# First tile of a two-layer convolution: plain load, TensorE transposes and a tap-by-tap product in place of transposing DMAs and product sums, with the shifts moved to ScalarE and a delayed GELU

## The chip, the cores and the metric

One core of a Trainium2 chip. The metric is the device time of the program in microseconds (us); every run here was in the fast state of the chip, so all runs may be compared. A profiled run also has a span, from the first to the last counted instruction, which is about 2 us shorter than its time. "Granted clock" is the share of TensorE's full clock that the records of the chip show for a stretch or a whole run.

Short names: PE is TensorE's matmul, PEld its weight load, DVE VectorE, ACT ScalarE, POOL GpSimd, SP an engine that here only issues DMAs. PSUM is the memory into which TensorE writes its products and from which VectorE and ScalarE read them. `L302` is line 302 of the kernel; a helper that issues all matmuls has one line, so tiles and operand names tell matmuls apart.

## The reference, cut to what matters

```python
# x: (2, 4000, 512), w1, w2: (5, 512, 512), g: (2, 8, 512), all bf16
h = sum(einsum("btc,cd->btd", pad(x)[:, i:i+T], w1[i]) for i in range(5))
h = gelu(h)[:, ::2]                      # only every second sample is kept
f = sum(einsum("btc,cd->btd", pad(h)[:, i:i+T1], w2[i]) for i in range(5))
f = gelu(f)[:, ::2]                      # (2, 1000, 512)
j = tanh((f @ w_f)[:, :, None] + (g @ w_g)[:, None])
out = j @ w_o                            # (2, 1000, 8, 512)
```

Both convolutions have five taps and stride 2. The kernel holds the samples in four phases, `xs[r]` with r = 0 to 3, where column c of phase r is sample 4c + r; one column then gives two outputs, sample 4c and sample 4c + 2. Direct, those two outputs take ten products (five taps each). The kernel takes seven: sums and differences of phases (a0, a1, a2, a3, b1, b3, and b2, which is phase 1 itself) are multiplied with taps or sums of taps, and the results are combined afterwards. Input channels come in four blocks of 128. A unit is 128 output channels of one tile: 28 matmuls in product form, 40 tap by tap. A tile has four units. The *epilogue* of a unit in product form is what VectorE and ScalarE do with its products: a copy that releases a PSUM bank (release copy), two combining operations, a pair sum and the GELU.

## The kernel before: what the change touches

```python
for ph in (2, 3, 1, 0):                     # first samples: DMA transposes of DRAM
    load_x(0, ph, 16, 272)
...                                         # cut: the other loads
def xf(src, off, dst, c0, n, which, eng):   # operands of the product form
    ph = lambda r, d: src[r, :, off + d:off + d + n]
    o = lambda kind: dst[kind, :, c0:c0 + n]
    if which == "a0":   tt(eng, o(0), ph(2, -1), ph(2, 0), sub)   # ph(2, -1): shifted
    elif which == "b3": tt(eng, o(3), ph(3, 0), ph(1, 0), sub)
    elif which == "b1": tt(eng, ph(3, -1), ph(3, -1), ph(1, 0), sub)
    elif which == "a3": tt(eng, o(2), ph(0, 1), ph(0, 0), sub)
    elif which == "a1": tt(eng, o(1), ph(0, 0), ph(2, 0), add)
    elif which == "a2": tt(eng, ph(0, 0), ph(2, 0), ph(0, 0), sub)
...
nxt = [(w, "pool" if w == "a3" else "dve") for w in ("b3", "a0", "b1", "a3", "a1", "a2")]
...
def post(self, m, where, between=()):       # after the matmuls of unit m
    act(c, ps.cols(C, n), ACT.Copy, scale=0.5)                    # release copy
    ...                                     # cut: two scalar_tensor_tensor on VectorE
    for f in between: f()                   # operands of the next tile
    tt("dve", tv, tv, ps.pair(A, step, n), add)                   # pair sum
    ...
    act(o, tv, ACT.Gelu_apprx_tanh)         # GELU follows at once
...
tiles = [Tile_(1, 0, xs[0], 16, ..., 250), Tile_(1, 0, xs[0], 266, ..., 250),
         Tile_(1, 0, xs[1], 12, ..., 250), Tile_(1, 0, xs[1], 262, ..., 250),
         Tile_(1, 1, xs[2], 16, ..., 500), Tile_(1, 1, xs[0], 12, ..., 500)]   # layer 1
```

Layer 1 is four tiles of 250 columns for batch 0 and two of 500 for batch 1; layer 2 is two tiles of 500. The rest (two projections, tanh, the output product) is the same in both kernels. PSUM has eight banks. A 250-column unit takes two of them and a 500-column unit four, handed out in turn by a counter `count["unit"]`. Helpers record every operation in program order and put in the waits; each engine runs its own operations in that order.

## Time and profile before

| | before |
|---|---|
| time, median (range, runs) | 314.73 us (314.15 to 315.94, 4) |
| span of the profiled run, granted clock | 312.4 us, 0.955 |
| chain that ended last: TensorE, VectorE, "issue" | 74%, 12%, 6% |
| TensorE busy | 280.3 us |
| second tile's first matmul; third tile; batch 1; layer 2 | 39.67; 55.03; 84.77; 137.88 us |

The page of the kernel before gives busy time (x is the number of instructions), then the span in 40 slices of 7.8 us, where a digit is the busy share in tenths (9 is 90% or more) and PEclk the granted clock in tenths.

```profile
PE 280.3 (90%) x1487; PEld 148.1 (47%) x1498; DVE 197.8 (63%) x262; ACT 128.4 (41%) x179; POOL 58.6 (19%) x41
...
PE   8259179959959999999998999999999999999995
...
POOL 1745000060199994004000000000000000000000
PEclk9959769998979999999999999999999999999999
...
PE 74%; DVE 12%; issue 6%; DMA 3%; ACT 3%; SPq 1%; DVEq 0%; ACTq 0%
```

TensorE is full from slice 13 on, at about 94 us. The holes, and the low clock, are all in the first third. The same stretch in windows (start:end, length, busy time of PE, PEld, DVE, ACT and POOL, granted clock, DMA share, GB/s):

```profile
8.28:18.78 10.50, 1.87 (x16) 1.49 (x17) 4.74 (x3) 0.00 (x0) 9.11 (x2) 0.80 1.12 264
18.78:34.00 15.22, 13.50 (x96) 10.67 (x96) 14.91 (x20) 0.38 (x1) 4.45 (x3) 0.80 1.14 184
34.00:42.65 8.65, 1.85 (x9) 1.04 (x9) 5.49 (x13) 2.75 (x6) 0.00 (x0) 0.56 0.81 172
42.65:54.90 12.25, 12.25 (x103) 10.73 (x104) 7.85 (x17) 3.74 (x8) 0.12 (x1) 0.89 0.20 45
54.90:68.00 13.10, 9.61 (x87) 8.04 (x85) 9.31 (x15) 2.80 (x6) 5.77 (x2) 1.00 1.00 263
68.00:89.00 21.00, 18.48 (x148) 15.11 (x148) 13.65 (x22) 4.76 (x10) 3.89 (x2) 0.92 0.39 113
```

The first number after the length is TensorE. From 8.28 to 18.78 us it worked 1.87 of 10.50 us, with 16 matmuls; from 34.00 to 42.65 it worked 1.85 of 8.65 us, at a clock of 0.56. VectorE, on the other hand, was busy 14.91 of 15.22 us in the second row: it was the engine that the first tile waited for. In the chain of waits of the same kernel the first 18 us read (start, us, what):

```profile
4.60 9.25 DMA xs_49<-in_x_dram
...
13.94 3.96 DVE xt_54 L283
```

So the second operand (b3, which needs two further phases; a0 was made at 7.45 us) had to wait for the transposing DMAs, 9.25 us of the chain, and the VectorE operation that makes it took 3.96 us beside GpSimd; one of the same size took 0.69 us without it. The timeline shows that stretching again at the first 500-column tile (start, us, engine, line, operation, operands and sizes, and in brackets how long the engine had been idle and what ended it):

```profile
83.53 1.19 DVE L283 TENSOR_TENSOR xt_54<-xs_51 128x2000 bf16<-128x2000 bf16 x1
...
85.11 3.52 POOL L283 TENSOR_TENSOR xt_55<-xs_49 128x2000 bf16<-128x2000 bf16 x1 [17.63 <-PE acc L294]
...
87.03 2.65 DVE L283 TENSOR_TENSOR xs_51<-xs_51 128x2000 bf16<-128x2000 bf16 x1
...
89.78 1.82 PE L294 MATMUL acc<-xs_51,w_t 128*128 128x500 bf16 x4 [3.14 <-issue]
```

A subtraction of 2000 bf16 elements takes VectorE 1.19 us. Started under a GpSimd operation it took 2.65 us: if it waited until GpSimd was done at 88.63, it then took 1.05 us, near its usual time. TensorE waited 3.14 us here; the profile names no releaser, but these matmuls read what the operation writes, and they start 0.10 us after its end. The Trainium skill, "SBUF — State Buffer", section "Who interferes with whom", says that a VectorE instruction with two SBUF inputs contends with a GpSimd instruction that reads SBUF, and that the one that comes second is blocked, not slowed. This trace agrees here. (The 3.96 us operation above ended 1.2 us before the record of the GpSimd operation beside it, so that case doesn't tell.)

### The profile page before, as it was taken

To read this page: it belongs to the slowest core of one execution; us is meant where nothing else is said; L and a number is where in the kernel's file an instruction comes from. 1 tells how busy PE (TensorE), PEld (TensorE's weight loads), DVE (VectorE), ACT (ScalarE), POOL (GpSimd) and SP (SyncE) were. 2 spreads that over 40 slices of the span, in tenths; PEclk is the share of its full clock that TensorE was granted. 3 is DMA by queue.
4 is the path that set the end of the run, shared out by engine and by line. 5 is a ranking of instruction groups with operands and counts; after the bars stand their busy time and mean duration, and the time that the engine had idled before them with its cause. 6 is when DMAs were issued, how large, how long until landed. Compare 5 with 4: busy or idle time off the path is not lost.

```text
span 312.4 us, 4021 instructions
## 1 busy us (share of the span) xinstructions
PE 280.3 (90%) x1487; PEld 148.1 (47%) x1498; DVE 197.8 (63%) x262; ACT 128.4 (41%) x179; POOL 58.6 (19%) x41
## 2 busy tenths in 40 slices
PE   8259179959959999999998999999999999999995
PEld 3147159848824434444443444444444444444442
DVE  0299775666678776768674324656767676767674
ACT  1000223221311223231324344876786786793840
POOL 1745000060199994004000000000000000000000
PEclk9959769998979999999999999999999999999999
DMA  8999940997000000000000000224444445444444
GB/s 220 297 183 177 228 106 3 201 342 200 2 0 1 0 2 0 0 2 0 1 0 2 0 0 0 69 81 154 153 153 152 148 147 162 151 153 151 151 153 135
DMA packets 58641, 31.87 MB, mean 102 GB/s; under 512 B 35950, under 2 KB 58622, under 8 KB 58622
## 3 DMA queue, kind: packets, MB, share of 16 engines
q1 hardware_dynamic: 55982, 29.00, 34.4%
q10 hardware_dynamic: 2640, 2.62, 2.7%
q8 instruction: 12, 0.20, 0.3%
q14 instruction: 7, 0.06, 0.1%
HBM read 6.82 MB, written 16.38 MB: 74 GB/s over the span
## 4 chain that ended last, share of the span: by engine, by line
PE 74%; DVE 12%; issue 6%; DMA 3%; ACT 3%; SPq 1%; DVEq 0%; ACTq 0%
PE acc L294 74%; DMA xs_49<-in_x_dram 3%; DVE xt_54 L283 2%; DVE w_t L283 1%; SPq L324 1%; DVE ty_65 L283 1%; DVE ty_66 L432 1%; DVE xs_49 L283 1%; ACT jT L287 1%; DVE ty_66 L283 1%; DVE ty_65 L432 1%; DVE xt_55 L283 1%; DVE w_sb L283 1%; ACT cs_64 L287 1%; DVE ty_67 L283 1%
## 5 line engine op out<-in xcount | busy, mean ns | idle before, releaser
L294 PE MATMUL acc<-wo_sb,jT 128*128 128x512 bf16 x489 | 107.5, 379 | 0.6
L294 PEld LDWEIGHTS acc<-wo_sb,jT 128*128 128x128 bf16 x500 | 48.8, 98 | 59.1 <-DVE ty_66 L283 0.3
L294 PE MATMUL acc<-xt_54,w_sb 128*128 128x250 bf16 (+1 forms) x256 | 50.6, 338 | 0.6 <-DVE xt_54 L283 0.6
L294 PE MATMUL acc<-xt_55,w_sb 128*128 128x250 bf16 (+1 forms) x256 | 49.6, 328 | 1.5 <-DVE xs_50 L283 1.3
L287 ACT ACTIVATE jT<-feT_77,geT 128x1000 bf16<-128x1000 f32 (+6 forms) x44 | 35.8, 890 | 0.0
L294 PEld LDWEIGHTS acc<-xt_54,w_sb 128*128 128x128 bf16 x256 | 26.4, 103 | 18.6 <-issue 2.1
L287 ACT ACTIVATE jT<-feT_76,geT 128x1000 bf16<-128x1000 f32 (+4 forms) x40 | 35.1, 948 | 0.0
L294 PEld LDWEIGHTS acc<-xt_55,w_sb 128*128 128x128 bf16 x256 | 25.4, 100 | 18.3 <-DVE xs_50 L283 1.6
L294 PE MATMUL acc<-xs_49,w_t 128*128 128x250 bf16 (+1 forms) x96 | 18.0, 316 | 9.3 <-DVE xt_54 L283 6.3
L294 PE MATMUL acc<-xs_49,w_sb 128*128 128x250 bf16 (+1 forms) x48 | 10.4, 364 | 8.6 <-DVE xs_49 L283 8.6
L287 ACT ACTIVATE cs_63<-acc 128x250 f32<-128x250 f32 (+1 forms) x16 | 7.5, 467 | 22.9 <-PE acc L294 22.9
L294 PEld LDWEIGHTS acc<-xs_49,w_t 128*128 128x128 bf16 x96 | 9.3, 100 | 14.9 <-DVE xt_54 L283 6.6
L283 DVE TENSOR_TENSOR xt_54<-xs_49 128x1000 bf16<-128x1000 bf16 x7 | 7.8, 1141 | 13.3 <-DMA xs_49<-in_x_dram 13.3
L573 DVE CAST ost_79<-acc 128x512 bf16<-128x512 f32 x11 | 7.6, 691 | 10.3 <-PE acc L294 10.3
L573 DVE CAST ost_85<-acc 128x512 bf16<-128x512 f32 x10 | 6.9, 692 | 10.4 <-PE acc L294 10.4
L432 DVE SCALAR_TENSOR_TENSOR ty_66<-acc,cs_64 128x250 f32<-128x250 f32 (+1 forms) x12 | 6.0, 544 | 11.1 <-ACT cs_64 L287 11.1
L287 ACT ACTIVATE ost_90<-acc 128x512 bf16<-128x512 f32 x10 | 6.0, 597 | 16.4 <-PE acc L294 16.4
L287 ACT ACTIVATE hT_61<-ty_65 128x500 bf16<-128x500 f32 x6 | 3.9, 658 | 21.0 <-DVE ty_65 L283 21.0
L432 DVE SCALAR_TENSOR_TENSOR ty_65<-acc,cs_63 128x250 f32<-128x250 f32 (+1 forms) x12 | 6.0, 542 | 9.5 <-ACT cs_63 L287 9.5
L294 PE MATMUL acc<-xs_51,w_t 128*128 128x500 bf16 x32 | 8.9, 404 | 3.1 <-issue 3.1
L294 PE MATMUL acc<-xs_50,w_t 128*128 128x250 bf16 x64 | 9.7, 274 | 2.1 <-DVE xt_55 L283 2.1
L379 POOL TENSOR_SCALAR w_t<-w_t 128x2048 bf16<-128x2048 bf16 x2 | 11.6, 5783 | 0.2
(98 smaller groups left out, 354.7 us busy)
## 6 DMA issues: line engine op xcount, KB each, us to landing
w_sb<-in_w_dram ACTq DMA_DIRECT2D x5, 512.0 KB, 7.7
w_sb<-in_w_dram SPq DMA_DIRECT2D x5, 512.0 KB, 6.4
out_dram<-ost_79 SPq DMA_DIRECT2D x11, 128.0 KB, 1.9
out_dram<-ost_83 SPq DMA_DIRECT2D x11, 128.0 KB, 1.9
out_dram<-ost_81 SPq DMA_DIRECT2D x10, 128.0 KB, 1.9
out_dram<-ost_87 SPq DMA_DIRECT2D x10, 128.0 KB, 1.9
out_dram<-ost_80 SPq DMA_DIRECT2D x9, 128.0 KB
out_dram<-ost_82 SPq DMA_DIRECT2D x9, 128.0 KB
```

The lines of the kernel that those rows point to most:

```text
L283: pl.op(eng, lambda e: e.tensor_tensor(out=o.ap, in0=a.ap, in1=b.ap, op=op), (a, b), (o,))
L287: pl.op("act", lambda e: e.activation(o.ap, i.ap, func, scale=scale, bias=0.0 if bias is None else bias.ap), rd, (o,))
L294: ins = e.matmul(o.ap, lhsT=l.ap, rhs=r.ap, start=start and n == 0, stop=stop and n == len(pairs) - 1, skip_group_check=not check)
L324: pl.dma("sp", lambda e: e.dma_start_transpose(out=dst.ap, in_=src), (), (dst,))
L379: pl.op(eng, lambda e: e.tensor_scalar(out=v.ap, in0=v.ap, scalar1=2.0, scalar2=None, op0=ALU.mult), (v,), (v,))
L432: pl.op("dve", lambda e, o=o, f=f: e.scalar_tensor_tensor(out=o.ap, in0=d.ap, scalar=f, in1=c.ap, op0=ALU.mult, op1=add), (d, c), (o,))
L573: pl.op("dve", lambda e, o=o, v=v: e.tensor_copy(out=o.ap, in_=v.ap), (v,), (o,))
```

## The change

The intent is to fill the first 138 us. Six things change together.

1. The first 256 columns come by a plain DMA, 128 groups of four samples at a time. TensorE transposes them in 32 steps into PSUM, and VectorE and ScalarE copy them out.
2. The first tile is convolved tap by tap (160 matmuls instead of 112), so it needs neither operands nor sums of weights nor an epilogue. VectorE makes the weight sums meanwhile.
3. The shifted operands a0, a3 and b1 are first copied by ScalarE (`shift`), so that VectorE reads aligned data. GpSimd no longer makes a3.
4. Batch 0's second half is one tile of 500 columns instead of two of 250.
5. The GELU of a unit is recorded after the next unit's release copy (`flush`).
6. GpSimd's preparation of layer 2's weights is cut into quarters, one recorded behind each unit of batch 1's first tile.

Smaller things come with these: the weights are loaded in the order of the taps, later samples are loaded only after the first ones, and b3 instead of b1 is the operand that is written in place.

The core of the diff; hunks and parts of hunks are left out where `# cut` stands.

```diff
+        first = [load_xr(rt) for rt in range(2)]
+        for i in (0, 4, 2, 1, 3):
+            load_w("act", w1_sb[i], w1[i].rearrange("(k c) d -> c k d", c=P))
# cut
-        warm_mm(22)
+        warm_mm(NWARM)        # NWARM = 16
+        psb = ps.h[:, :].bitcast(BF16)
+        for rt in range(2):
+            for pp in range(2):
# cut: bank 4 + 2 * rt + pp, eight transposes e.transpose(..., ident)
+                if pp:
+                    act(o, pv, ACT.Copy)
+                else:
+                    pl.op("dve", lambda e, o=o, pv=pv: e.tensor_copy(out=o.ap, in_=pv.ap), (pv,), (o,))
# cut
+        def shift(src, off, dst, c0, n, which):
+            r, d, kind = {"a0": (2, -1, 0), "a3": (0, 1, 2), "b1": (3, -1, 3)}[which]
+            act(dst[kind, :, c0:c0 + n], src[r, :, off + d:off + d + n], ACT.Copy)
# cut
-                tt(eng, o(0), ph(2, -1), ph(2, 0), sub)
+                tt("dve", o(0), o(0), ph(2), sub)
# cut: a3 and b1 alike
+                tt("dve", ph(3), ph(3), ph(1), sub)      # b3, now in place
# cut
-        count = {"unit": 0}
+        count = {"unit": 2}
# cut
                 act(c, ps.cols(C, n), ACT.Copy, scale=0.5)
+                flush()
+                for f in scal:
+                    f()
# cut
                 tt("dve", tv, tv, ps.pair(A, step, n), add)
-                act(o, tv, ACT.Gelu_apprx_tanh)
+                pending.append(lambda: self.gelu(m, tv))
# cut
-                 Tile_(1, 0, xs[1], 12, xt[1], 0, 500, 250), Tile_(1, 0, xs[1], 262, xt[1], 250, 750, 250),
+                 Tile_(1, 0, xs[1], 12, xt[1], 0, 500, 500),
# cut
+        for i in (0, 4, 2, 1, 3):
+            for m in range(NK):
+                for s in range(2):
+                    r, d = tap_at[i][s]
+                    mm(ps.cols(m * NT + 256 * s, n),
+                       [(w1_sb[i, k, m * P:(m + 1) * P], xs[0][r, k, 16 + d:16 + d + n]) for k in range(NK)],
+                       i == 0 and s == 0, i == 3, False)
# cut: weight sums on VectorE
+        for w in ("a0", "b1", "a3"):
+            tiles[1].shift(w)
+        for w in ("a0", "b1", "b3", "a3", "a1", "a2"):
+            tiles[1].xf(w)
```

## The prediction

> **What bounds it now.** The chain of waits gives TensorE 74% of the 312.4 us span, but windows show two halves. At the end TensorE is busy 109.6 of 113.4 us; a 500-column unit of 28 matmuls takes 5.9 us. From layer 2's start (137.9 us in the timeline) to the end is 174.5 us, which the change hardly touches. The first 137.9 us hold only four 500-column tiles (94.5 us). About 43 us are lost: 30 until the second tile starts (39.7/42.65 us: eight DMA transposes issuing over 16.8 us, 12 VectorE weight sums of 0.69 us, VectorE operations stretched to 2.2 us beside GpSimd), 7.5 to 84.8 us, 6 to 137.9 us.
>
> The Trainium skill, "TensorE: Matmul & The Clock Gate", "Part 1: The HAM clock gate", says the array drops to half clock after an idle window of about 3.4 us, until one busy window. The trace agrees: granted clock 0.50 from 16 to 24 and 36 to 44 us, and even after a 2.1 us gap at 66 us.
>
> **What changes, costed (estimates from the trace).**
> - First samples: 1 MB plain beside the weights. DMA moved 232-360 GB/s from 2 to 12 us, so they land at 7-9 us; 16 transposes (1-1.7 us) and a 1.1-1.2 us copy follow. Convolution starts near 11 us.
> - Tap by tap: 160 matmuls of 250 columns instead of 112: 17.1 instead of 12 us, plus about 2 at half clock, as TensorE has holes from 6 to 11 us. Ends at 29-30 us. Weight sums run under it. No VectorE epilogue: four GELUs of 0.65 us.
> - Second tile: in-place b3 writes cells that the last tap reads, so b3, a3, a1 (0.6-0.7 us each) run only after the convolution: a gap near 2.1 us and probably a slow window (+1.7). Starts near 32 us.
> - It needs VectorE for 4 x 1.4 + 6 x 1.19 = 12.8 us against 12 us of TensorE, and ScalarE shifts of 1.95 us (0.83 ns per element) precede the next copy. The third tile, now 500 columns, takes PSUM banks just used, so I expect 2-3 us of stall and another slow window. It starts at 47-48 us.
> - Then three tiles at 23.6 us. GpSimd leaves the operands; its weight preparation (about 24 us) still runs beside VectorE, which has about 43 of 47 us in those tiles: 1-2 us of stall.
> - Delayed GELU and ScalarE copies: 12.6 of 23.6 us of ScalarE per 500-column tile, off the path. Aligned VectorE operands gain nothing: shifted and unshifted subtractions both take 0.6-0.69 us.
>
> **Sum.** 47.5 + 1.7 + 3 x 23.6 + 1 = 121 us for layer 2's start instead of 137.9; plus 174.5 gives a 295.5 us span, about 297 us as time (2.1 more). Without the two stalls and slow windows: 289. I say 295 us, range 288 to 302.
>
> **What would show it.** First convolution matmul at 10-12 us; its 160 matmuls over 17-20 us; then a VectorE-caused gap of about 2 us; VectorE-caused idling before the third tile; layer 2's first matmul at 115-124 us; from there 174-175 us.
>
> **What would make it wrong.** Plain loads landing after 10 us, or taps 1 and 3 after their turn; half clock through most of the tap-by-tap convolution (up to +8 us); transposed loads for the third tile arriving after 48 us; contention with GpSimd or ScalarE's order delaying 500-column tiles; or the transition stalls hidden (289 or less). A result within 2% would need about 13 us more of losses.
>
> Faster by over 2%: 0.94; within 2%: 0.05; slower: 0.01.

## The result, and the profile after

The changed kernel takes 292.55 us (290.94 to 293.93, 4 runs) against 314.73 us: a ratio of 0.9289, with a 95% interval of 0.9233 to 0.9344. A ratio here is the mean time of one kernel's runs over that of the other's of the same rounds, so not quite the ratio of the medians quoted.

The profiled run of the changed kernel is the slowest of its four, 293.93 us, with a span of 292.1 us and a clock of 0.988. Its page, the same lines:

```profile
PE 280.4 (96%) x1460; PEld 141.6 (48%) x1460; DVE 182.3 (62%) x237; ACT 158.0 (54%) x187; POOL 33.1 (11%) x39
...
PE   8897987999999999999989999999999999999995
...
POOL 1000000099994000000000000000000000000000
PEclk9999797999999999999999999999999999999999
...
PE 92%; DVE 3%; issue 2%; ACT 1%; POOL 0%; DVEq 0%; ACTq 0%; POOLq 0%
```

TensorE was busy as long as before (280.4 us) in a span 20 us shorter. Its share of the chain rose from 74% to 92%. Two dips are left, at slices 5 and 7 of the PEclk row. The windows (columns as before) show what they are:

```profile
0.00:9.91 9.91, 7.43 (x49) 3.88 (x49) 1.98 (x3) 3.42 (x4) 1.50 (x18) 1.00 0.83 289
9.91:27.23 17.32, 17.31 (x160) 15.50 (x160) 9.98 (x15) 4.88 (x6) 0.00 (x0) 1.00 1.17 237
27.23:29.25 2.02, 0.01 (x1) 0.01 (x1) 1.89 (x4) 0.59 (x1) 0.00 (x0) 1.00 1.01 225
29.25:33.00 3.75, 3.75 (x20) 2.76 (x21) 1.22 (x3) 1.05 (x2) 0.00 (x0) 0.54 1.15 164
33.00:43.04 10.04, 10.03 (x95) 8.97 (x92) 8.70 (x13) 6.80 (x8) 0.12 (x1) 1.00 0.69 143
43.04:45.62 2.58, 0.00 (x1) 0.01 (x1) 2.52 (x5) 0.66 (x1) 0.00 (x0) 1.00 0.46 106
45.62:50.00 4.38, 4.38 (x13) 1.71 (x14) 0.00 (x0) 1.53 (x3) 0.00 (x0) 0.61 1.50 210
50.00:118.15 68.15, 68.15 (x325) 31.48 (x323) 50.77 (x53) 33.19 (x31) 31.46 (x20) 1.00 0.24 68
```

The tap-by-tap convolution ran from 9.91 to 27.23 us without a hole and at full clock. Then TensorE stood still for 2.02 us while VectorE was busy for 1.89 of them, and worked the next 3.75 us at a clock of 0.54. The same happened once more at the third tile: 2.58 us still, then 4.38 us at 0.61. From 50.00 to 118.15 us it was busy all of 68.15 us. A stretch of low clock ("slow window" below) costs 3.75 x (1 - 0.54) = 1.7 us, or 4.38 x (1 - 0.61) = 1.7 us.

The timeline names what ended the two gaps, and shows the two ScalarE copies out of PSUM, which end at 9.81 us, 0.10 before the convolution's first matmul (VectorE's two, 0.69 us each, were done by 9.01):

```profile
7.87 1.94 ACT L295 ACTIVATE xs_49<-acc 128x1024 bf16<-128x1024 bf16 x2 [1.32 <-PE acc L363]
...
29.25 1.00 PE L302 MATMUL acc<-xs_49,w_t 128*128 128x250 bf16 x4 [2.02 <-DVE xt_54 L291]
...
44.89 0.67 DVE L291 TENSOR_TENSOR ty_67<-ty_67,acc 128x500 f32<-128x500 f32 x1
45.62 1.15 PE L302 MATMUL acc<-xs_50,w_t 128*128 128x500 bf16 x4 [2.58 <-DVE ty_67 L291]
```

The first gap waits for operands of the second tile (`xt_54`), the second for the last pair sum of the second tile (`ty_67`), which still reads a PSUM bank that the third tile wants. These two waits are the subject of the first three experiments.

Where the 20.3 us of the span went, from the first matmuls of each stage in the two timelines:

| stretch | before | after | saved |
|---|---|---|---|
| start to the end of the second tile's matmuls | 55.03 | 43.04 | 12.0 |
| from there to the first matmul of batch 1 | 29.74 | 27.89 | 1.9 |
| batch 1 of layer 1, to layer 2's first matmul | 53.11 | 47.22 | 5.9 |
| layer 2 to the end | 174.5 | 173.95 | 0.6 |

Two 500-column tiles are 224 matmuls; the 47.22 us of the third row are what TensorE needs for them alone (0.21 us each at full clock). Nothing is left to gain in that row. What remains are the two gaps with their slow windows, and the start.

### The profile page after: what moved, and what is told of

It reads as the page before. It is cut to its first block, busy times and chain, and to the rows that moved or that the text cites. A ratio compares the mean times of both kernels' runs of the same rounds, so it can differ in the third digit from the quotient of the medians.

```text
span 292.1 us, 3892 instructions
## 1 busy us (share of the span) xinstructions
PE 280.4 (96%) x1460; PEld 141.6 (48%) x1460; DVE 182.3 (62%) x237; ACT 158.0 (54%) x187; POOL 33.1 (11%) x39
## 4 chain that ended last, share of the span: by engine, by line
PE 92%; DVE 3%; issue 2%; ACT 1%; POOL 0%; DVEq 0%; ACTq 0%; POOLq 0%
PE acc L302 92%; ACT xt_55 L295 1%; DVE ty_69 L291 1%; PE acc L363 1%; DVE xt_54 L291 0%; DVE xt_55 L291 0%; DVE ty_68 L486 0%; DVE ost_86 L626 0%; DVE ty_67 L291 0%; DVE ty_68 L291 0%; DVE ty_69 L486 0%; DVE ty_67 L486 0%; POOL zero L288 0%; ACT cs_65 L295 0%; ACT cs_66 L295 0%
## 5 line engine op out<-in xcount | busy, mean ns | idle before, releaser
L302 PE MATMUL acc<-xt_55,w_sb 128*128 128x500 bf16 x160 | 38.3, 374 | 0.0
L302 PE MATMUL acc<-xt_54,w_sb 128*128 128x500 bf16 (+1 forms) x160 | 33.8, 347 | 0.0
L295 ACT ACTIVATE cs_65<-acc 128x500 f32<-128x500 f32 (+1 forms) x12 | 6.6, 553 | 37.8 <-PE acc L302 37.8
L302 PE MATMUL acc<-xs_49,w_sb 128*128 128x250 bf16 (+1 forms) x192 | 23.7, 278 | 1.2 <-issue 1.2
L302 PEld LDWEIGHTS acc<-xt_55,w_sb 128*128 128x128 bf16 x160 | 15.7, 98 | 18.4 <-issue 0.5
L302 PEld LDWEIGHTS acc<-xt_54,w_sb 128*128 128x128 bf16 x160 | 16.0, 100 | 13.4
L302 PEld LDWEIGHTS acc<-xs_49,w_sb 128*128 128x128 bf16 x192 | 18.6, 97 | 4.8 <-issue 1.3
L295 ACT ACTIVATE cs_66<-acc 128x500 f32<-128x500 f32 (+1 forms) x12 | 6.6, 552 | 25.2 <-PE acc L302 25.2
L302 PE MATMUL acc<-xs_49,w_t 128*128 128x250 bf16 (+1 forms) x64 | 13.6, 339 | 2.0 <-DVE xt_54 L291 2.0
L295 ACT ACTIVATE ost_93<-acc 128x512 bf16<-128x512 f32 x10 | 6.0, 597 | 16.4 <-PE acc L302 16.4
L291 DVE TENSOR_TENSOR ty_69<-ty_69,acc 128x1000 f32<-128x1000 f32 (+1 forms) x8 | 9.0, 1128 | 6.2 <-PE acc L302 6.2
L291 DVE TENSOR_TENSOR ty_68<-ty_68,acc 128x1000 f32<-128x1000 f32 (+1 forms) x8 | 9.0, 1128 | 6.1 <-PE acc L302 6.1
L295 ACT ACTIVATE ost_87<-acc 128x512 bf16<-128x512 f32 x10 | 5.9, 593 | 11.4 <-PE acc L302 11.4
L291 DVE TENSOR_TENSOR ty_67<-ty_67,acc 128x1000 f32<-128x1000 f32 (+1 forms) x8 | 8.5, 1060 | 4.1 <-PE acc L302 4.1
L486 DVE SCALAR_TENSOR_TENSOR ty_68<-acc,cs_65 128x500 f32<-128x500 f32 x8 | 5.1, 674 | 7.4 <-PE acc L302 7.4
```

The lines of the kernel that those rows point to most:

```text
L291: pl.op(eng, lambda e: e.tensor_tensor(out=o.ap, in0=a.ap, in1=b.ap, op=op), (a, b), (o,))
L295: pl.op("act", lambda e: e.activation(o.ap, i.ap, func, scale=scale, bias=0.0 if bias is None else bias.ap), rd, (o,))
L302: ins = e.matmul(o.ap, lhsT=l.ap, rhs=r.ap, start=start and n == 0, stop=stop and n == len(pairs) - 1, skip_group_check=not check)
L486: pl.op("dve", lambda e, o=o, f=f: e.scalar_tensor_tensor(out=o.ap, in0=d.ap, scalar=f, in1=c.ap, op0=ALU.mult, op1=add), (d, c), (o,))
```

## The experiments

Twelve kernels ran, all with correct results, each timed against the kernel before on the same chip. Every difference below is from the changed kernel unless said otherwise. Because the calls used different chips, "difference" in the table is the difference of two ratios, times 314.7 us.

| edit to the changed kernel | median us (range, runs) | ratio (95%) | difference |
|---|---|---|---|
| none | 292.55 (290.94 to 293.93, 4) | 0.9289 (0.9233 to 0.9344) | 0 |
| PSUM banks in another order | 289.40 (288.53 to 290.51, 6) | 0.9199 (0.9170 to 0.9228) | -2.8 |
| b3 last | 290.37 (289.72 to 291.01, 6) | 0.9232 (0.9207 to 0.9256) | -1.8 |
| both | 286.50 (286.07 to 287.29, 5) | 0.9108 (0.9085 to 0.9131) | -5.7 |
| GELU at once | 299.82 (298.76 to 301.16, 6) | 0.9531 (0.9501 to 0.9560) | +7.6 |
| no ScalarE shifts | 290.18 (289.78 to 292.81, 6) | 0.9247 (0.9210 to 0.9284) | -1.3 |
| DMA-transposed first samples | 296.14 (294.49 to 297.55, 4) | 0.9415 (0.9369 to 0.9461) | +4.0 |
| products in the first tile, banks and b3 as in "both" | 290.35 (289.98 to 290.77, 4) | 0.9230 (0.9200 to 0.9259) | -1.9 |
| third tile as 2 x 250 | 299.97 (297.92 to 300.74, 6) | 0.9528 (0.9496 to 0.9560) | +7.5 |
| the same, preparation later in the program | 299.68 (297.42 to 300.24, 6) | 0.9511 (0.9481 to 0.9540) | +7.0 |
| the same, preparation held back | 295.83 (294.11 to 296.62, 6) | 0.9370 (0.9335 to 0.9404) | +2.5 |
| a3 on GpSimd | 293.63 (293.21 to 295.06, 5) | 0.9342 (0.9319 to 0.9365) | +1.7 |
| "both", no shifts, 13 warm-up matmuls | 285.78 (285.35 to 286.00, 5) | 0.9084 (0.9065 to 0.9103) | -6.5 |

The changed kernel's own interval is wide, and the clock of its runs says why: 293.93 us at 0.988, 292.78 at 0.993, 292.33 at 0.994, 290.94 at 0.998. About 0.006 of clock is one slow window (1.7 of 290 us). By that measure two, one, one and none of them fell into these runs. Where an interval overlaps, runs of equal clock are compared below.

### The wait before the third tile: another order of PSUM banks

```diff
-        count = {"unit": 2}
+        count = {"unit": 0}
```

With the counter at 2 the second tile's units take banks 4-5, 6-7, 0-1 and 2-3, and the third tile's first unit takes banks 0 to 3, which the last two units have just filled. With 0 the second tile ends in banks 4 to 7.

> The PSUM bank counter starts at 0 instead of 2, nothing else. Theory (bank reuse): the third tile's first products take banks 0 to 3, which the second tile's last two units had just used, so TensorE waits 2.58 us for the last pair sum (43.04 to 45.62 us) and then runs a slow window. With the counter at 0 those banks are free earlier, TensorE waits only for the tile's last operand a2: stall at or below 0.5 us, no slow window there, 3.5 to 4.5 us faster than the changed kernel (about 288 us, ratio to before about 0.916). Rival (VectorE is the limit of the second tile, 12.8 us of work, whatever banks are used): the stall moves to a wait for a2 of about 2 us and the gain is under 1 us.

Measured: 289.40 us, 2.8 us less. Windows of this kernel, around the gap after the first tile and around the third tile:

```profile
27.74:29.80 2.06, 0.01 (x1) 0.04 (x2) 1.93 (x4) 0.59 (x1) 0.00 (x0) 1.00 1.13 225
29.80:34.00 4.20, 4.20 (x24) 3.21 (x25) 2.10 (x4) 1.99 (x2) 0.00 (x0) 0.59 1.07 182
43.00:46.00 3.00, 2.98 (x18) 1.47 (x16) 2.75 (x5) 1.37 (x3) 0.00 (x0) 1.00 0.35 80
```

The third tile's stall of 2.58 us is gone and its slow window with it (2.98 of 3.00 us busy, clock 1.00); the gap after the first tile is as it was. That the stall was a matter of banks is shown. The six runs also show what a slow window costs: three at clock 0.994 took 290.17, 290.39 and 290.51 us, three at 1.000 took 288.53, 288.56 and 288.62. The mean difference is 1.8 us. So the gap of about 2.06 us, which every run should have, seems to be followed by a slow window in some runs and not in others; only the profiled run (290.17 us) shows the gap and the window themselves.

### The gap after the first tile: the in-place operand last

```diff
-        for w in ("a0", "b1", "b3", "a3", "a1", "a2"):
+        for w in ("a0", "b1", "a3", "a1", "a2", "b3"):
             tiles[1].xf(w)
```

The second tile's b3 is written over phase 3, whose cells the last tap of the first tile reads at the tile's border, so b3 can only run after the convolution. In the given order a3 and a1 queue behind it. The columns themselves don't overlap (the taps read columns 15 to 265 of phase 3, b3 writes 266 to 515): the helper that puts in the waits keeps its books in cells of 32 bytes, which is 16 columns, and the border falls inside one. So the wait comes from the bookkeeping; finer cells were not tried.

> The second tile's six VectorE operand operations in another order: b3 last instead of third, so only b3 has to wait for the last tap. Theory: the 2.02 us gap after the first tile (27.23 to 29.25 us) and the slow window after it (1.65 us more for 20 matmuls) are the price of b3's in-place write ahead of a1; the second tile then starts at 27.3 us and all later work comes 3 to 4 us earlier (about 289 us, ratio about 0.918). Rival: the epilogue of the first tile or ScalarE's GELUs hold TensorE there, or the third tile's start is fixed by something else (its data); then under 1 us is gained.

Measured: 290.37 us, 1.8 us less by the ratios, though the intervals overlap. The profile is clearer: TensorE's piece of the chain runs from 9.49 without a break for 27.57 us, through the convolution into the second tile, so the gap is gone; but the third tile's stall grew from 2.58 to 3.04 us, with a slow window, and five of six runs have a clock of 0.993 or 0.994. Part of the gain was handed on to the next wait.

### Both together

The two edits above.

> Both edits together. Theory: the two losses are in series and add: 7 to 8 us faster than the changed kernel, about 285 us, ratio about 0.905. Rival: they share a bound (VectorE's chain through the second tile), so both together gain hardly more than the better one alone.

Measured: 286.50 us, ratio 0.9108, clock 0.999 to 1.000 in all five runs. The expected size was missed by about 1.5 us: 5.7 to 6.0 us came, not 7 to 8. In the changed kernel's slowest run the two gaps (4.6 us) and their slow windows (3.4) sum to 8.0 us, but its median run has only one slow window, so 6.3 us was to be had on the median. In addition, TensorE now waits 0.8 us at 41.6 us:

```profile
41.08 1.19 DVE L291 TENSOR_TENSOR xs<-xs 128x2000 bf16<-128x2000 bf16 x1
41.59 0.59 ACT L295 ACTIVATE cs<-acc 128x500 f32<-128x500 f32 x1 [0.38 <-PE acc L302]
...
42.37 1.00 PE L302 MATMUL acc<-xs,w_t 128*128 128x500 bf16 x4 [0.82 <-ACT cs L295]
```

The profile puts the wait down to ScalarE's release copy, but that copy reads another bank, and ScalarE had itself just waited 0.38 us for TensorE. What these matmuls read is a2, which VectorE finished at 42.27. Earlier in this trace the second unit's release copy, at 33.03 us, stood behind two shift copies (29.51 to 33.03), and VectorE waited 1.34 us for it; this probably made a2 late. The range shrank from 3.0 to 1.2 us, and the clock no longer varies from run to run. This settles the two waits as the cause of nearly all that the changed kernel loses after its start.

### GELU behind the next copy, undone

```diff
-                pending.append(lambda: self.gelu(m, tv))
+                self.gelu(m, tv)
```

> The GELU of a unit is issued at once after its pair sum, as before the change, instead of behind the next unit's copy. Theory: in 500-column units the copy comes 1.7 us after the unit starts and the GELU is done by 2.4 us, so nothing on the path moves there; only in the second tile, where VectorE and ScalarE are short, it costs 0 to 2.5 us (292 to 295 us). Rival (the delayed GELU is a main part of the gain): 5 us or more slower.

Measured: 299.82 us, 7.6 us more. My theory, that ScalarE has so much room that the order does not matter, fell; the rival won. Even at equal clock the loss is 5 to 6 us (299.76 us at 0.987 against 293.93 at 0.988). About 0.8 us of that may be chance: in the profiled run the warm-up lasted longer and the convolution started at 10.72 instead of 9.91 us. Two timelines of the third tile, first this kernel with the GELU at once, then the changed kernel:

```profile
56.03 1.20 DVE L291 TENSOR_TENSOR ty<-ty,acc 128x1000 f32<-128x1000 f32 x1 [1.00 <-PE acc L302]
...
57.26 1.11 ACT L295 ACTIVATE hT<-ty 128x1000 bf16<-128x1000 f32 x1 [1.33 <-DVE ty L291]
...
58.27 0.56 ACT L295 ACTIVATE cs<-acc 128x500 f32<-128x500 f32 x1
...
58.94 1.26 DVE L486 SCALAR_TENSOR_TENSOR ty<-acc,cs 128x500 f32<-128x500 f32 x2 [1.71 <-ACT cs L295]
```

```profile
53.42 1.20 DVE L291 TENSOR_TENSOR ty_68<-ty_68,acc 128x1000 f32<-128x1000 f32 x1 [1.00 <-PE acc L302]
...
55.10 0.59 ACT L295 ACTIVATE cs_66<-acc 128x500 f32<-128x500 f32 x1 [1.98 <-PE acc L302]
...
55.59 1.11 ACT L295 ACTIVATE hT_61<-ty_68 128x1000 bf16<-128x1000 f32 x1
...
55.95 1.26 DVE L486 SCALAR_TENSOR_TENSOR ty_69<-acc,cs_66 128x500 f32<-128x500 f32 x2 [1.33 <-PE acc L302]
```

Above, ScalarE stands idle until the pair sum (`ty`) is done, runs the GELU for 1.11 us, and only then the release copy (`cs`) of the next unit; VectorE, which waits for that copy, is idle 1.71 us. The four steps pair sum, GELU, copy, VectorE form a loop in which each waits for the one before. Below, the copy starts as soon as TensorE is done with it, and the GELU runs behind it while VectorE already works. The busy time of ScalarE is the same (157.2 and 158.0 us). In the kernel with the GELU at once the third tile's stall is 4.63 us instead of 2.58, TensorE waits another 1.79 us at 101.3 us, in the 500-column tiles, where the changed kernel shows no wait, and layer 2's mid-point (the projection of g) comes at 154.21 instead of 149.12 us. So ScalarE was never short of time; its order was on the critical path.

### The shifts on ScalarE, undone

```diff
-                tt("dve", o(0), o(0), ph(2), sub)
+                tt("dve", o(0), ph(2, -1), ph(2), sub)
 (a3 and b1 alike; all calls of shift removed)
```

> No shifted copies by ScalarE: VectorE subtracts straight from the operands shifted by one column, and writes where it wrote before. Theory: VectorE takes 0.60 to 0.69 us per 1000 and 1.19 us per 2000 elements with shifted or aligned operands alike, so the copies bought nothing: within 1 us of the changed kernel (291.5 to 293.5 us, ratio 0.926 to 0.932), ScalarE's busy time 20 us lower. Rival (the change's own reason: a bfloat16 operand that starts at an odd column makes VectorE slow): the three shifted subtractions take about twice as long, VectorE falls behind in the second tile, 3 us or more slower.

Measured: 290.18 us. The interval overlaps the changed kernel's, and at equal clock there is no difference: 292.51 and 292.81 us at 0.993 against 292.33 and 292.78. ScalarE's busy time fell by 29 us, to 128.7; I had expected 20. One group of VectorE operations, summed over the profile (count, busy us, mean ns, idle before), first without the ScalarE copies, with operands shifted by one element, then from the changed kernel with aligned ones:

```profile
L291 DVE TENSOR_TENSOR xt<-hT 128x2000 bf16<-128x2000 bf16 x8 | 9.4, 1194 | 0.0
```

```profile
L291 DVE TENSOR_TENSOR xt_54<-xt_54,hT_61 128x2000 bf16<-128x2000 bf16 x3 | 3.5, 1193 | 0.0
```

1194 against 1193 ns. The aligned copies buy nothing, as the prediction said. Six of the eight operations of the first group have a shifted operand (two are the unshifted a1), so a penalty would show in its mean.

### The plain load, undone

```diff
-        first = [load_xr(rt) for rt in range(2)]
+        first = ()
+        for ph in (2, 0, 3, 1):
+            load_x(0, ph, 16, 272)
 (the TensorE transposes and their copies removed)
```

> The first samples by DMA transposes again (phases 2, 0, 3, 1), without TensorE's transposes and their copies; tap-by-tap convolution and all else as changed. Theory: tap by tap needs only phases 2 and 0 at first, and in the old trace the first transposed phase was in at 7.4 us and they followed each 2.1 us, so the convolution starts at about 10 us as well, later phases come before their taps, and only a slow window may follow the idle time after the warm-up: 292 to 296 us. Rival (my prediction: the plain load is what moves the start): the convolution starts at 16 us or later, 5 us or more slower.

Measured: 296.14 us, 3.6 us more by medians and 4.0 by ratios, between what theory and rival had said. The timeline of TensorE's first matmuls:

```profile
7.59 0.59 PE L302 MATMUL acc<-xs,w_sb 128*128 128x250 bf16 x4 [0.30 <-DMA xs<-in_x_dram]
12.40 4.83 PE L302 MATMUL acc<-xs,w_sb 128*128 128x250 bf16 x28 [4.21 <-DMA xs<-in_x_dram]
```

The convolution starts 2.3 us earlier than with the plain load, waits 4.21 us for the second phase, and then has a slow window (clock 0.58 from 12.40 to 16.00). The second tile starts at 32.99 instead of 29.25 us. In the kernel before, TensorE's second group of operands was not ready before 18.78 us: b3 and b1 needed the third phase to land, in by 13.94 us, and two VectorE operations, of which the first took 3.95 us beside GpSimd. Tap by tap, TensorE eats phases as they land, with no VectorE operation between. That this is why the same transposes cost less here is read from the two traces, not tested. The two parts of the change may thus partly do the same job, and the load alone is worth 4 us on top of the other.

### The first tile in product form

The plain load kept; the first tile's operands, weight sums, 112 matmuls and epilogue as before, and banks and b3 as in the kernel with both edits, which is its fair base.

```diff
-        for i in (0, 4, 2, 1, 3):            (the 160 tap-by-tap matmuls)
+        for which in ("a0", "b3", "b1", "a3", "a1", "a2"):
+            xf_old(*t0.a, which)
+        wsum13(w1_sb, w1_t, "dve")
...
+            t0.post(m, (m * NT, (4 + m) * NT, (4 + m) * NT + 256, 256), [lambda w=w: tiles[1].xf(w) for w in ws])
```

> Plain load and TensorE transposes kept, but the first tile computed by products with its epilogue, as before the change (all operand operations and weight sums on VectorE). Theory: VectorE has 3.9 us of operands and 10.2 us of weight sums before the last product, then 9.4 us of epilogue and second-tile operands, so the second tile starts at 30 to 33 us instead of 29.3: 1 to 4 us slower in spite of 48 matmuls less. Rival (the tap-by-tap form only costs TensorE 5 us): 3 us or more faster.

Measured: 290.35 us. Neither range held, since I had not allowed for the banks and the order that came with it: against the changed kernel it is 1.9 us faster. Against its base it loses 0.9230 - 0.9108 = 0.0122, or 3.8 us. Its timeline has TensorE's last matmul of the first tile end near 25.2 us, about 2 us before the tap-by-tap one ends in the changed kernel, then a wait of 3.37 us for VectorE, which still makes pair sums, and a slow window. The saved 48 matmuls are paid back in VectorE's epilogue. Tap by tap costs TensorE 5 us more and is still the better form here, where the next tile waits for VectorE. Other orders of that epilogue were not tried.

### The third tile as two of 250 columns

```diff
-                 Tile_(1, 0, xs[1], 12, xt[1], 0, 500, 500),
+                 Tile_(1, 0, xs[1], 12, xt[1], 0, 500, 250), Tile_(1, 0, xs[1], 262, xt[1], 250, 750, 250),
 (the b1 shift of both made at once; later steps keep their tile)
```

> The third tile as two tiles of 250 columns again (the b1 shift of both is made at once, as b3 of the first overwrites a column that the second one's needs). Theory: TensorE takes the same time per column, and the stall before the first 500-column tile (banks just used, 2.6 us and a slow window) only moves one tile later: 291 to 294 us. Rival (the longer tile is itself a part of the gain, by fewer fixed costs per VectorE instruction): 3 us or more slower; or, if the stall belongs to VectorE's load in the second tile, which is now lighter (9.6 us instead of 12.8), 3 us or more faster.

Measured: 299.97 us, 7.5 us more; the theory was wrong. There is no stall at the third tile (0.20 us), but a longer one comes later. This is the timeline of the 500-column tile that follows, and of a pair of VectorE operations before it:

```profile
62.20 4.08 DVE L291 TENSOR_TENSOR xt<-xt,xs 128x2000 bf16<-128x2000 bf16 x2
...
74.93 1.85 PE L302 MATMUL acc<-xs,w_t 128*128 128x500 bf16 x4 [7.58 <-DVE ty L291]
```

In product form a 250-column tile gives TensorE 12 us of work, in which VectorE has the epilogue and the next, 500-column tile's operands to do. Two operations of 2000 elements took 4.08 us here, beside GpSimd's weight preparation; 2.30 us is what they take otherwise.

### The same with the preparation later

First the preparation was moved one tile later in the program (`qi == 5` instead of 4, as the tiles are now numbered).

> The run with two 250-column tiles (300.0 us), with GpSimd's weight preparation one tile later (at the second 500-column tile of layer 1, instead of at the first; it then still ends before layer 2). Theory: of the 7.6 us stall before the first 500-column tile the greater part came from GpSimd running beside VectorE in a 250-column tile that had 12.8 us of VectorE work for 12 us of TensorE already; without it the stall falls to about 2.5 us, as in the changed kernel: 293 to 296 us. Rival (VectorE's own load, or ScalarE's order, made the stall): it stays over 5 us and the time within 2 us of 300.

Measured: 299.68 us, and the preparation started at 58.58 us, no later than in the others. Nothing stands ahead of it in GpSimd's queue, and its weights have landed, so a later place in the program delays nothing. This run tested nothing of the theory. Then a GpSimd operation that waits for the first unit of the first 500-column tile was put before the preparation.

```diff
+                if qi == 4 and m == 0:
+                    memset(warm[:])
+                    pl.ops[-1].deps["pe"] = max(o.idx for o in pl.ops if o.eng == "pe")
```

> The run before this left the weight preparation where it was (GpSimd's queue has nothing ahead of it that would hold it; it began at 58.6 us in both), so it told nothing. Here GpSimd waits, ahead of the preparation, for the first unit of the first 500-column tile; otherwise the kernel with two 250-column tiles. Theory as before: GpSimd's contention made most of the 7.2 to 7.6 us stall and the slow clock after it; without it the stall before the first 500-column tile is 2 to 3.5 us and the time 293 to 297 us. Rival (VectorE's own load, or ScalarE's shifted copies ahead of the next unit's copy, made the stall): over 5 us of stall, 298 us or more.

Measured: 295.83 us, 5.0 us less by ratios than with the preparation in its way. The stall fell from 7.58 to 3.60 us, and the pair of operations took 2.30 us. More than half of the loss of the 250-column form is thus contention between VectorE and GpSimd; the rest, 2.5 us above the changed kernel, holds a stall 1.0 us longer than the 2.58 it replaces and a later start of the convolution (10.66 against 9.91 us), and was not separated further. The 500-column tile earns its place mainly by what it lets VectorE do while GpSimd works.

### One operand back on GpSimd

```diff
-                tt("dve", o(2), o(2), ph(0), sub)
+                tt("pool", o(2), src[0, :, off + 1:off + 1 + n], ph(0), sub)
 (the shift of a3 removed)
```

> Operand a3 of every tile but the first by GpSimd again, in one operation and without its ScalarE copy; all else as in the changed kernel. Theory (contention): VectorE's operand operations beside it stretch from 1.19 us to about 2 us, the second tile has no slack for that, and the third starts later: 293 to 297 us. Rival (VectorE is relieved of one operation per tile, which pays for it): 290 to 292.5 us.

Measured: 293.63 us. The intervals overlap, so the time is not separated; at clock 0.994 these runs are about 1 us slower (293.2 to 293.8 against 292.3 and 292.8). The mechanism shows in the timeline:

```profile
28.13 3.87 POOL L291 TENSOR_TENSOR xt<-xs 128x2000 bf16<-128x2000 bf16 x1 [7.12 <-DVE xs L291]
28.67 3.88 DVE L291 TENSOR_TENSOR xs<-xs 128x1000 bf16<-128x1000 bf16 x1
```

A VectorE operation that takes 0.68 us took 3.88, until GpSimd was through with its own. TensorE waited 1.43 and 2.88 us in the second tile. The third tile's stall became shorter, 1.30 us; VectorE had one operation less to do before it, which may be why the total moves so little.

### A version that beats both

Banks and b3 as above, no ScalarE shifts, and 13 warm-up matmuls instead of 16. The 16 of the other kernels took from 5.08 to 6.45 us, by how early the clock came up, and the transposes stand behind them. The trace doesn't show that 13 are quicker: they took 5.71 us, and the convolution started at 9.98 us, against 9.49 to 10.72 in the other kernels with the plain load and the tap-by-tap form.

> The candidate: bank counter at 0, b3 last in the second tile, no shifted copies by ScalarE, and 13 instead of 16 warm-up matmuls (in several runs the warm-up, not the data, held the first transposes). Theory: both stalls and their slow windows gone (286.5 us with the first two edits), ScalarE's order no longer ahead of the third tile's first copy (0.8 us), the convolution starts 0.5 to 1 us earlier on average: 284.5 to 286.5 us, ratio 0.904 to 0.911. Rival: with less warm-up the clock stays low into the convolution, 1 to 3 us slower than 286.5.

Measured: 285.78 us (285.35 to 286.00), ratio 0.9084 with an interval of 0.9065 to 0.9103. TensorE is busy 98% of the span. Its chain of waits is nearly one piece:

```profile
9.98 30.95 PE acc L302 x280
...
40.94 98.84 PE acc L302 x468
...
141.06 139.71 PE acc L302 x664
```

What is left are 1.2 us before the convolution, 1.3 us before the projection of g (a pair sum that holds a PSUM bank), and the start. Against the kernel with both edits it gains 0.7 us by medians; which of its two additions gave it was not separated, though the 0.8 us wait is gone: a2 is done at 40.84 us, before TensorE wants it.

## Why the prediction was right, point by point

It said 295 us within 288 to 302; 292.55 us came. The changed kernel is 22 us faster for the reason given: the losses of the first 138 us were taken away, and the second half did not move. Part of the nearness of 295 is luck. The prediction's own sum, with both stalls and both slow windows, was about 297 us; 295 leans toward its 289 without them, and no step of the sum gives it. The profiled run, which has both stalls and both slow windows, took 293.93 us, 3 us less than that sum.

| term of the sum | predicted | measured |
|---|---|---|
| convolution's first matmul | near 11 us | 9.91 us |
| its 160 matmuls | 17.1, plus about 2 at half clock | 17.3, none at half clock |
| gap before the second tile | near 2.1, "probably a slow window (+1.7)" | 2.02, and 1.7 |
| third tile's stall | 2 to 3, and a slow window | 2.58, and 1.7 |
| third tile starts | 47 to 48 us | 45.62 us |
| stall in the 500-column tiles | 1 to 2 | 0 |
| layer 2's first matmul | 115 to 124 us | 118.15 us |
| from there to the end | 174 to 175 | 173.95 |

Right, and tested: both transition stalls and their causes (VectorE's order in the second tile and PSUM banks just used), by removing each alone and both. "Aligned VectorE operands gain nothing" held too (1194 and 1193 ns).

Mis-sized, all on the slow side: the convolution's start, where the second half of the samples was in by 7.67 us, low in the predicted 7 to 9, its 16 transposes took 1.06 us and the ScalarE copy that ended last 1.02, not 1.1 to 1.2; the 2 us of half clock in the convolution, since the idle time of 1.18 us before it was not followed by a slow window; and the 1 to 2 us of stall in the 500-column tiles. VectorE's operations were stretched beside GpSimd there too, 1.87 us instead of 1.19 on the mean for one group, but they were not what TensorE waited for. The two slow windows were counted as certain; over the four runs they came, by the clocks, two, one, one and no time, so the median holds one.

Wrong, without harm to the sum: "Delayed GELU and ScalarE copies: 12.6 of 23.6 us of ScalarE per 500-column tile, off the path." The share of busy time was read as slack. Undoing the delay cost 7.6 us. The GELU is off the path because it is delayed; in place, it stands between the pair sum and the next release copy. The sum survived, because it priced the changed kernel with the delay in it, but by the same reasoning the expectation of that experiment put the loss at 0 to 2.5 us.

Over-attributed: "eight DMA transposes issuing over 16.8 us" stood first among the causes of the 30 us. With tap-by-tap products behind them, those transposes cost only 4 us more than the plain load. What made them costlier in the kernel before was, by its trace, the VectorE work between them and TensorE, 3.3 us of it lost beside GpSimd; no run tests this alone.

What the runs did not show: how the 12.0 us saved up to the second tile divide exactly. The plain load is worth 4.0 us and the tap-by-tap form 3.8 us, each with the other present, in two kernels with different waits after them; the rest (VectorE no longer sharing with GpSimd in the second tile, weight sums out of the way) was not measured alone, and the parts overlap. Nor was item 6 of the change, the weight preparation in quarters, undone alone, or the order of the loads.

## What to carry to other kernels

- A TensorE gap of 2 us can cost nearly 4: the gap and a slow window behind it. In a tuned kernel look for the gaps at changes of tile shape first, and ask of each which in-place write or which PSUM bank it waits for; here two edits of one line each gave 5.7 us.
- On an engine that runs in order, the place of an operation decides, not the engine's share of busy time. Put work whose input comes late (a GELU) behind the copy for which the next unit waits, and delay side work by a dependence; a later place in the program does nothing where the queue ahead is empty.
- A better form of one stage is worth what the next stage can use: 48 fewer matmuls lost 3.8 us, because they needed an epilogue on the engine for which the next tile waited.

## What the Trainium skill lacked or had wrong

- "TensorE: Matmul & The Clock Gate", "Part 1: The HAM clock gate" and "HAM oscillation — how this bites in real kernels": the half clock is said to follow an idle window of about 3.4 us, and the rule drawn is to have no idle gaps longer than that. That is too lax here. Gaps of 2.02 and 2.58 us were followed by 3.75 and 4.38 us at a clock of 0.54 and 0.61. The section says that the window runs freely, which fits that a 2.06 us gap seems to have brought a slow window in three of six runs of one kernel and not in the others (clocks 0.994 and 1.000, 1.8 us apart), and that a gap of 2.24 us before the third tile brought none in two other traces. Gaps of 1.18, 1.30, 1.79 and 1.95 us were not followed by one. An idle window of 3.4 us doesn't fit into a gap of 2 us, so the measurement decides. The page has no figure for gaps shorter than about 3 us.
- "VectorE: DVE Perf Modes", "Mode 2×_1P": it lists an alignment of 4 bytes as required; "What auto-detection actually checks" names only 16-bit tensors and a step of one. The runs agree with the second: a group with six of eight operands shifted by one bf16 element took 1194 ns per 2000 elements, an aligned one 1193. So the page is at odds with itself, and the first passage is the one to mend.
- "SBUF — State Buffer", "Who interferes with whom": agrees; it gives ratios (6.8 and 1.5 times) and no durations from a kernel. Here a VectorE subtraction of 0.68 us took 3.88 us beside one GpSimd operation of 3.87 us.
- No page that I read says what a GELU placed ahead of a release copy on ScalarE costs: 7.6 us of 292.55, at the same busy time of ScalarE (157.2 and 158.0 us).
